# Pacing of block attention under two pair passes of a mixture-of-experts kernel: two end marks moved

## The chip, the cores and the metric

The kernel runs on one core of one Trainium2 chip. The metric is the device time of one execution in microseconds (us); the time before is the median of three runs.

## The reference

Attention over a batch of 4, 8 heads, 768 positions and head dimension 64. Each query sees the keys less than 16 positions away and 24 block summaries (for each block of 32 positions, the largest of K and the mean of V). The result is the x of four experts whose outputs are mixed for each token.

```python
k_sum = k.reshape(B, H, nb, block, D).max(axis=3)
v_sum = v.reshape(B, H, nb, block, D).mean(axis=3)
...
scores_all = np.concatenate([scores_l_m, scores_s], axis=-1)
...
a = a / (np.sum(a, axis=-1, keepdims=True) + 1e-09)
v_all = np.concatenate([v, v_sum], axis=2)
return np.matmul(a, v_all).astype(np.float32)
...
for e in range(E):
    h = np.maximum(x @ w1[e], 0.0)
    out += p[:, e:e + 1] * (h @ w2[e])
```

x has 3072 rows of 512, w1 is 512 by 1024 and w2 1024 by 512 for each expert.

## The kernel before, in words

**Tokens.** The 3072 tokens are eight blocks of 384 (a batch is two blocks). Attention is cut into 64 pieces: 96 queries of four heads, 16 pieces to a batch. Pieces 0 to 7 come ahead of everything else. Pieces 8 to 63 are issued between the matmuls of the experts.

**A piece** is a chain of steps: `load_piece` (line 286, two DMAs, kr and qv), `stage_a` (295, operands split into high and low parts by ACT and POOL), `scores` twice (328: matmuls into psc, masked maximum on DVE, exponential on ACT), `probs` (360, DVE and ACT make aw), `transposed` (386, a DMA transpose), `values` (392, matmuls into px) and `to_x` (429: ACT and DVE make xs, a DMA writes it to DRAM as xd). For each of the batches 1 to 3, `setup_k` (220) and `setup_v` (228) make the block summaries: four K chunks and four V chunks are loaded into two chunk buffers, reduced on DVE, and scaled and turned (`stack_v`, 239).

**Experts.** A plan (line 1071) has six passes: block 0 with experts 0 and 1, block 1 with experts 1 and 0, blocks 0 and 1 together with experts 2 and 3, and then three pair passes, each with one batch and all four experts. In a pair pass each expert has a first stage (`pair_units`, 970: four groups of seven products of six matmuls, whose sums ACT and DVE finish in PSUM while PE goes on) and a second stage (`second`, 907: 144 matmuls into po). In the first pair pass the scaled and split weights are made for the first time (`w1_operands`, 813, and `w2_scaled`, 776, on ACT, POOL and DVE) and stored to DRAM; the second and third pair passes load them from there.

**x of the next pair.** When the last second stage of a pass begins, `x_operands` (453) starts on the x of the next batch. It has four parts of 96 tokens. A part is loaded (xr, into one of the two chunk buffers) once its four xd are written, and ACT, POOL and DVE split it into the 14 operand tiles. The tiles are those that the pass before used, so a tile is free when its last matmul is done.

**The order.** Every step has a key, a place in units of pieces (lines 1033 to 1050). From piece 16 on, piece n has k = n + 1.12; its `stage_a` stands at k - 0.6, its `to_x` at k + 2.3. The summaries of batch b stand at 16b + 1.12 - 2.0 (K) and, for b = 2 and 3, - 1.3 (V). Each pass has an end mark in `ENDS` (line 36), and `advance` issues all steps whose key lies below a mark that moves from the end of the pass before to the end of this one with the work done:

```python
paced = len(experts) * (first_us * (SLOW if pair else 1.0) + second_us)
...
for us, pace in units:
    issue_deferred()
    u += us
    done += us * pace
    advance(pos + (end - pos) * min(1.0, done / paced))

    if nxt < NTB // 2 and u > whole - second_us + 1e-3:
        if parts is None:
            xpair[nxt], parts = x_operands(nxt)
        if parts and written.get((nxt, TB // QB - len(parts))) == 4:
            parts.pop(0)()
```

In a pair pass first_us is 29.4 and second_us 33.264 for one expert and SLOW is 0.6, so paced is 4 x (17.64 + 33.264) = 203.6. The order in which the program issues is a priority only: from line 1067 on a scheduler that models the engines in time places the instructions on each engine's queue, and it may take a later one first where an earlier one isn't ready. Two kinds stay in program order: the K and V chunk loads (line 203) and what was issued before line 1067. Every engine then runs its own queue in order. All DMAs named here are issued by SP. Nearly every instruction carries line 75, that of a helper, so the rows below are told apart by tile names.

Of the kernel before, what the change touches and what calls it, by code (L numbers as in the profile page):

```python
# [32 lines left out]
NEG = -1.0e9 / SCALE  # L33

SHIFT = 1.12
ENDS = (17.52, 25.5, 38.0, 53.0, 68.0, 70.0)
WARM = 11

KEYS = (1.38, 3.85, 1.13, 11.28, 5.91, 6.72, 13.44, 18.09, 21.41, 52.74, 24.82, 23.32, 21.81, 24.25, 59.33, 71.64, 6.83, 9.12)
# [23 lines left out]
def attn_moe(ctx: ExitStack, tc: tile.TileContext, qvL, qv0, v0L, kD, kT, vT, w1L, w2L, dpL, cst, out):  # L63
# [1008 lines left out]
    pos = per  # L1072
    for (tbs, experts), end in zip(plan, ENDS):
        pair = tbs if isinstance(tbs, int) else None
# [89 lines left out]
```

## Time and profile before

| | us |
|---|---|
| runs before: median (lowest to highest) | 1180.99 (1179.97 to 1182.93) |
| profiled execution, device time | 1185.18 |
| its span, first to last instruction | 1183.40 |
| PE busy in the span | 1116.8 (94%) |
| mean granted TensorE clock | 0.972 of full speed |

The page shows one execution. PE is TensorE's matmuls, PEld its weight loads, DVE VectorE, ACT ScalarE, POOL GpSimd, SP the queue that issues the DMAs. In timelines an instruction's idle time ahead of it stands in brackets with what ended it. The first, second and third pair pass begin at 392.08, 693.21 and 945.79 us by PE's first product of each; the last matmul ends near 1179.5.

### The profile page before, as it was taken

To read this page: it belongs to the slowest core of one execution; us is meant where nothing else is said; L and a number is where in the kernel's file an instruction comes from. 1 tells how busy PE (TensorE), PEld (TensorE's weight loads), DVE (VectorE), ACT (ScalarE), POOL (GpSimd) and SP (SyncE) were. 2 spreads that over 40 slices of the span, in tenths; PEclk is the share of its full clock that TensorE was granted. 3 is DMA by queue.
4 is the path that set the end of the run, shared out by engine and by line. 5 is a ranking of instruction groups with operands and counts; after the bars stand their busy time and mean duration, and the time that the engine had idled before them with its cause. 6 is when DMAs were issued, how large, how long until landed. Compare 5 with 4: busy or idle time off the path is not lost.

```text
span 1183.4 us, 19188 instructions
## 1 busy us (share of the span) xinstructions
PE 1116.8 (94%) x6562; PEld 716.4 (61%) x6562; DVE 702.8 (59%) x1767; ACT 595.1 (50%) x1682; POOL 448.2 (38%) x554
## 2 busy tenths in 40 slices
PE   9899698999999879899987999999999999999998
PEld 7888587898897544454544555555555454545453
DVE  5887779875889765665867754453545440414141
ACT  5767466664557777767646654453424230303030
POOL 2588456772736667565544521212111100000000
PEclk9999788999999899899998999999999999999999
DMA  6476656663845767757758354555543132423201
GB/s 237 140 224 177 176 147 184 165 169 92 255 104 151 228 219 228 239 192 208 252 191 227 94 158 125 154 167 155 150 123 83 60 128 67 129 80 116 83 21 54
DMA packets 172179, 181.92 MB, mean 154 GB/s; under 512 B 79664, under 2 KB 115504, under 8 KB 172080
## 3 DMA queue, kind: packets, MB, share of 16 engines
q1 hardware_dynamic: 172080, 180.69, 52.4%
q8 instruction: 51, 0.84, 0.3%
q14 instruction: 48, 0.39, 0.1%
HBM read 129.66 MB, written 34.08 MB: 138 GB/s over the span
## 4 chain that ended last, share of the span: by engine, by line
PE 47%; DMA 2%; DVE 2%; POOL 1%; SPq 1%; ACT 0%; issue 0%; ACTq 0%; DVEq 0%
PE po L75 24%; PE phb L75 10%; PE pha L75 6%; PE phc L75 3%; PE phd L75 3%; PE psc L75 1%; PE px L75 1%; DMA wr<-in_w2L 1%; SPq L75 1%; DMA kch<-in_kT 0%; DMA vch<-in_vT 0%; DVE vsr L75 0%; DVE vmax L75 0%; DMA qv<-in_qvL 0%; POOL qs L75 0%
## 5 line engine op out<-in xcount | busy, mean ns | idle before, releaser
L75 PE MATMUL po<-w,hh 128*128 128x512 f16 (+1 forms) x1536 | 465.1, 384 | 1.3 <-DVE acc L75 1.3
L75 PE MATMUL po<-w,hl 128*128 128x512 f16 (+1 forms) x768 | 293.7, 384 | 0.0
L75 PEld LDWEIGHTS <-w1g 128*128 128x128 f16 x2016 | 197.0, 99 | 157.5 <-issue 28.1
L75 PEld LDWEIGHTS <-hh 128*128 128x128 f16 x1152 | 109.6, 98 | 126.6 <-issue 1.6
L75 PE MATMUL phb<-xh_t,w1g 128*128 128x384 f16 x576 | 166.8, 333 | 14.0 <-DVE phc L75 5.9
L75 PE MATMUL ph<-xh,w 128*128 128x384 f32 x512 | 143.1, 350 | 9.0 <-ACT xh L75 3.7
L75 POOL TENSOR_TENSOR ks<-kr,ks 128x304 fp32r<-128x304 f32 x112 | 100.4, 901 | 131.1 <-ACT ks L75 130.3
L75 POOL TENSOR_TENSOR w<-wr,w 128x512 fp32r<-128x512 f32 (+1 forms) x76 | 101.6, 1343 | 77.8 <-ACT w L75 72.5
L75 ACT ACTIVATE ms<-ms,nb 96x152 f32<-96x152 f32 x256 | 104.2, 414 | 25.2 <-DVE nb L75 24.0
L75 PE MATMUL pha<-xh,w1g 128*128 128x384 f16 x384 | 109.1, 332 | 4.0 <-DVE nb L75 2.5
L75 DVE SCALAR_TENSOR_TENSOR acc<-po,pw,acc 128x512 f32<-128x512 f32 x72 | 51.6, 743 | 90.3 <-PE po L75 90.2
L75 PEld LDWEIGHTS ph<-xh,w 128*128 128x128 f32 x512 | 96.9, 196 | 11.6 <-ACT xh L75 4.0
L75 DVE CUSTOM_DVE_ANT_0 ms<-psc,c_sb 96x152 f32<-96x152 f32 x256 | 69.4, 305 | 57.1 <-PE psc L75 54.2
L75 PEld LDWEIGHTS <-hl 128*128 128x128 f16 x576 | 56.3, 98 | 67.2
L75 PE MATMUL phb<-xl_t,w1g 128*128 128x384 f16 x288 | 96.0, 333 | 0.0
L75 PE MATMUL ph<-xl,w 128*128 128x384 f32 x256 | 88.3, 345 | 0.0
L75 POOL TENSOR_TENSOR v<-qv,v 128x256 f16<-128x256 f32 (+1 forms) x56 | 43.3, 775 | 113.7 <-ACT v L75 88.7
L75 PEld LDWEIGHTS po<-w,hh 128*128 128x128 f32 x384 | 71.1, 190 | 14.5
L75 PE MATMUL psc<-ks,qs 128*96 128x152 f32 x448 | 65.8, 272 | 12.6 <-DVE nb L75 5.4
L75 ACT CAST w<-wr 128x512 fp32r<-128x512 f32 (+1 forms) x100 | 60.7, 615 | 32.8 <-DMA wr<-in_w1L 22.8
L75 DVE TENSOR_TENSOR aw<-ms,aw 96x512 f16<-96x512 f32 x112 | 65.4, 617 | 14.6 <-ACT aw L75 14.4
L75 ACT CAST aw<-ms 96x512 f16<-96x512 f32 x112 | 49.4, 489 | 48.1 <-issue 28.9
(153 smaller groups left out, 1854.6 us busy)
## 6 DMA issues: line engine op xcount, KB each, us to landing
wr<-in_w1L SPq DMA_DIRECT2D x76, 256.0 KB, 3.6
wr<-in_w2L SPq DMA_DIRECT2D x72, 256.0 KB, 3.3
qv<-in_qvL SPq DMA_DIRECT2D x56, 320.0 KB, 3.4
kr<-in_kD SPq DMA_DIRECT2D x56, 256.0 KB, 3.2
w1g<-wdg SPq DMA_DIRECT2D x28, 512.0 KB, 3.5
w<-wd SPq DMA_DIRECT2D x48, 256.0 KB, 2.7
w1g<-wdg SPq DMA_DIRECT2D x28, 384.0 KB, 3.7
wdg<-w1g SPq DMA_DIRECT2D x16, 512.0 KB, 3.7
```

The lines of the kernel that those rows point to most:

```text
L75: ins = getattr(self.engine, name)(*a, **kw)
```

## The change

It moves the end marks of the first and the second pair pass. Nothing else is touched.

```diff
-ENDS = (17.52, 25.5, 38.0, 53.0, 68.0, 70.0)
+ENDS = (17.52, 25.5, 38.0, 51.6, 67.3, 70.0)
```

The first pair pass goes from mark 38.0 to 51.6 where it went to 53.0: 13.6 places where it was 15. The second goes from 51.6 to 67.3 where it went from 53.0 to 68.0. The last step of all, `to_x` of piece 63, has key 63 + 1.12 + 2.3 = 66.42, so the second pass really issues 14.82 places where it issued 13.42. The third pass has no attention in either kernel.

## Rows read from the trace of the kernel before

**Rows 1.** The page of the profile: span, busy time of each engine, and the span in 40 slices of 29.6 us: busy tenths of PE and tenths of the granted TensorE clock.

```profile
span 1183.4 us, 19188 instructions
...
PE 1116.8 (94%) x6562; PEld 716.4 (61%) x6562; DVE 702.8 (59%) x1767; ACT 595.1 (50%) x1682; POOL 448.2 (38%) x554
...
PEclk9999788999999899899998999999999999999999
```

**Rows 2.** Busy time of each engine in the three pair passes (first, second, third), cut at the first matmul of each. Columns: stretch, its length, busy us of PE, PEld, DVE, ACT, POOL (x instructions), granted clock as a share of full speed, DMA share, GB/s.

```profile
392.08:693.21 301.13, 270.17 (x1556) 143.90 (x1556) 199.41 (x477) 200.06 (x551) 168.32 (x213) 0.95 0.68 207
693.21:945.79 252.58, 251.63 (x1514) 136.20 (x1513) 123.28 (x324) 105.26 (x312) 47.61 (x69) 1.00 0.46 131
945.79:1179.50 233.71, 233.68 (x1249) 121.99 (x1247) 68.51 (x124) 42.56 (x96) 0.00 (x0) 1.00 0.28 85
```

**Rows 3.** Who PE waited for in the first pair pass. Columns: us in total, times, longest us.

```profile
PE phb L75 <- DVE phc L75: 5.9, 3, 2.3
PE psc L75 <- DVE nb L75: 5.4, 1, 5.4
PE phb L75 <- ACT phb L75: 4.6, 3, 2.3
PE psc L75 <- POOL qs L75: 2.8, 1, 2.8
PE psc L75 <- DVE hl L75: 2.6, 2, 2.2
PE pha L75 <- DVE nb L75: 2.5, 3, 1.9
```

**Rows 4.** Busy time in two stretches of 10 us of the first pair pass, columns as in Rows 2.

```profile
620.00:630.00 10.00, 3.44 (x18) 2.04 (x20) 7.42 (x23) 6.11 (x16) 2.73 (x3) 0.63 0.75 189
630.00:640.00 10.00, 9.12 (x55) 5.13 (x51) 6.42 (x12) 6.04 (x19) 6.57 (x8) 0.86 0.89 224
```

**Rows 5.** Groups of instructions of the second pair pass that belong to the attention: xcount | busy us, mean ns | idle before, releasers. A piece has two of ks, four of ms with its accumulator, two of aw, and one of each of the others.

```profile
L75 ACT ACTIVATE ms<-ms,nb 96x152 f32<-96x152 f32 x48 | 19.9, 414 | 1.2 <-DVE nb L75 0.7
...
L75 ACT CAST aw<-ms 96x512 f16<-96x512 f32 (+1 forms) x24 | 10.4, 482 | 15.3 <-issue 13.1 <-DVE ms L75 1.1 <-ACT p L75 0.9
...
L75 ACT CAST ks<-kr 128x304 fp32r<-128x304 f32 x22 | 9.8, 445 | 19.7 <-PE psc L75 19.7
...
L75 ACT ACTIVATION_READ_ACCUMULATOR ms<-ms,nb 96x1 f32 x48 | 9.0, 187 | 0.0
...
L75 ACT CAST qs<-qv 128x384 fp32r<-128x384 f32 x11 | 5.6, 510 | 0.0
...
L75 ACT ACTIVATE qv<-qv,vscale 128x256 f32<-128x256 f32 x10 | 5.1, 508 | 14.9 <-DMA qv<-in_qvL 14.9
...
L75 ACT ACTIVATE xs<-px 128x192 f32<-128x192 f32 x14 | 4.6, 332 | 7.2 <-PE px L75 7.2
L75 ACT CAST v<-qv 128x256 f16<-128x256 f32 x11 | 4.5, 408 | 19.6 <-PE px L75 19.6
```

**Rows 6.** The chain that ended last, the stretch of the last expert's second stage: start, us, what.

```profile
1154.65 24.84 PE po L75 x115
```

**Rows 7.** DMA issues of SP around the summary of the last batch (kch and vch are its four K and four V chunks). Columns: start, us, instruction, count; an issue that lasts long was waiting.

```profile
574.85 0.90 SPq L203 DMA_DIRECT2D kch<-in_kT  x2
...
592.82 7.79 SPq L203 DMA_DIRECT2D vch<-in_vT  x4
604.30 0.33 SPq L75 DMA_DIRECT2D wr<-in_w2L  x1
```

**Rows 8.** PE at the start of the fourth expert's first stage: start, us, instruction, and in brackets the idle time before it with what ended it.

```profile
618.03 0.34 PE L75 MATMUL pha<-xh,w1g 128*128 128x384 f16 x1
...
624.57 0.92 PE L75 MATMUL psc<-ks,qs 128*96 128x152 f32 x4 [5.39 <-DVE nb L75]
627.38 0.48 PE L75 MATMUL pha<-xh,w1g 128*128 128x384 f16 x1 [1.88 <-DVE nb L75]
```

**Rows 9.** ACT in the same place.

```profile
624.62 0.72 ACT L75 ACTIVATE wr<-wr,scalew 128x512 f32<-128x512 f32 x1 [3.71 <-DMA wr<-in_w2L]
```

**Rows 10.** SP before the second pair pass: the last write of x (xd) for it and the last two loads of x (xr).

```profile
661.43 0.53 SPq L75 DMA_DIRECT2D xd<-xs  x1
667.58 0.81 SPq L75 DMA_DIRECT2D xr<-xd  x2
```

**Rows 11.** DVE: the last instruction of the split of x for the second pair pass.

```profile
680.04 0.59 DVE L75 TENSOR_TENSOR xl_t<-xr,xh_t 128x192 f16<-128x192 f32 x2
```

**Rows 12.** The split of x: durations ns min/median/max, first and last start us, form.

```profile
L75 DVE TENSOR_TENSOR xr<-xr x48: 335/438/1146, 348.8 to 934.9; 128x192 f32<-128x192 f32 x48
...
L75 POOL TENSOR_TENSOR xl<-xr,xh x36: 542/550/1002, 347.7 to 930.2; 128x192 f16<-128x192 f32 x36
```

**Rows 13.** DMA issues by line: KB each, median us from issue to landing.

```profile
xd<-xs SPq DMA_DIRECT2D x48, 96.0 KB, 2.1
xr<-xd SPq DMA_DIRECT2D x12, 384.0 KB, 3.4
```

**Rows 14.** SP before the third pair pass: the last two writes of x and the last two loads of x.

```profile
908.00 5.56 SPq L75 DMA_DIRECT2D xd<-xs  x2
923.75 0.82 SPq L75 DMA_DIRECT2D xr<-xd  x2
```

## The prediction

> **What bounds the kernel now.** I read the page first: PE is busy for 1116.8 of 1183.4 us and its clock falls only in places [rows 1]. Then the busy time by pass. The second and third pair passes are PE without gaps: 251.63 busy of 252.58 us, 233.68 of 233.71, at full clock. The first is not: 270.17 of 301.13, so 30.96 us idle, at a mean clock of 0.95 [rows 2]. All three do the same expert matmuls, so the difference is attention and loss. A piece costs PE (251.63 - 233.68) / 13 = 1.4 us (the second pass holds 12 sets of scores and 14 of values, so some 13). The first pass has about two pieces more, 2.8 us. So 301.13 - 252.58 - 2.8 = **45.7 us of the first pair pass is loss**: 30 us idle, the rest matmuls at the low clock. Where PE idles for long the clock follows: in the 10 us with 3.44 us of PE work the mean is 0.63, in the next 0.86 [rows 4].
>
> What PE waits for there is mixed: products waiting for DVE and ACT to finish the sums in PSUM (phc 5.9, phb 4.6), and attention: scores or a shared bank waiting for nb, qs and hl, 5.4 + 2.8 + 2.6 + 2.5 = 13.3 us of 30.96, or 43% [rows 3]. No engine is full: DVE and ACT have 199 and 200 us in 301 [rows 2]. They run in order, and in the first stages weight splitting, attention and the PSUM sums share them. So it is a matter of crowding, and there are fewer pieces to crowd after the change.
>
> **The change part by part.** Nothing is removed or added. 1.4 places (15 - 13.6) go from the first pass to the second, each with its steps on five queues: on PE 1.4 us, on ACT 2 x 0.445 + 4 x (0.414 + 0.187) + 2 x 10.4/24 + 0.510 + 0.508 + 0.332 + 0.408 = 5.9 us [rows 5], on SP two loads, a transpose and a write, on DVE and POOL at most (123.28 - 68.51)/13 = 4.2 and 47.61/13 = 3.7 us [rows 2].
>
> PE's own 1.4 x 1.4 = 2.0 us only changes pass: zero. In the second pass ACT's 1.4 x 5.9 = 8.3 us goes beside PE: ACT is at 105 of 253 us, DVE at 123, POOL at 48, and PE loses 0.95 us in the pass [rows 2]. I cost it at nothing. If that cover failed, a piece would cost what one costs now in the first pass, 45.7 / 15 = 3.0 us, and 1.4 pieces 4.3 us: what is gained would come back.
>
> In the first pass the gain isn't shown by any row, so I bound it. Low: only the waits named for attention shrink with the number of pieces, 43% of 45.7 us x 1.4/15 = 1.8 us. High: ACT limits throughout, and all its 8.3 us comes off. A loss is not excluded (the second rival). Between, I let the whole loss go with the number of pieces: 45.7 x 1.4/15 = **4.3 us**. I take it because idle time and slow clock come together [rows 4], while ACT at two thirds busy [rows 2] speaks against the high end.
>
> The summaries of the last batch (keys 47.12 and 47.82) stay in the first pass but move within it: from (47.12 - 38)/15 = 0.608 to 9.12/13.6 = 0.671, and from 0.655 to 0.722. The third expert's second stage runs from 0.587 to 0.75, so they stay inside it; cost zero, and a rival if that fails.
>
> The x of the next pair is complete later. For the second pass the last write moves from (50.42 - 38)/15 = 0.828 to 12.42/13.6 = 0.913; the last second stage begins at 0.837. That is 0.0853 x 203.6 = 17.4 units. Of these 15.6 lie in that stage, whose 33.264 units take 144 x 24.84/115 = 31.1 us [rows 6]: 14.6 us. 1.8 lie in the first stage before it, whose 17.64 units take 233.71/4 - 31.1 = 27.3 us [rows 2]: 2.8 us. Together 17.4 us. Before, the last write was issued at 661.43, the loads waited until 667.58 [rows 10] and the split ended at 680.6 [rows 11], 12.6 us ahead of 693.21 [rows 2]. After, in the same time frame: write 678.8, 2.1 to land, 3.4 for the load [rows 13], and one part's split, between half and all of the 12.2 us that two parts took from the end of their loads' issue (668.4) less that load: 4.4 to 8.8. Sum 688.7 to 693.1: **just in time**, cost zero. For the third pass the shift is 14.82/15.7 - 13.42/15 = 0.0493, x 203.6 x 31.1/33.264 = 9.4 us. The last write there came by 913.6 and the loads only at 923.75 [rows 14]; after: 923.0 + 2.1 + 3.4 + 8.8 = 937.3 against 945.79 [rows 2]. Zero too.
>
> One rule speaks against this. In the split, DVE's subtractions on xr take between 335 and 1146 ns for one form, and POOL's beside them 542 to 1002 [rows 12]. The Trainium skill ("SBUF — State Buffer", section "SBUF: two separate sides") has VectorE instructions with two inputs in SBUF and GpSimd instructions share one port pair by an exclusive lock, and the loser waits for the whole instruction. The spread in those rows agrees. By that rule attention that is now issued beside the last split would lengthen it and the sum would be that of the first rival; by the medians alone it stays at 4.3 us.
>
> **Sum.** Profiled execution 1185.18 (1183.40 of span and 1.78 around it) - 4.3 = 1180.9. It stands 4.2 us above the median of 1180.99, so the median becomes **1176.7 us**.
>
> **The rivals.** *x comes late.* The split's seven two-operand DVE instructions each stand behind one POOL instruction of 0.55 us [rows 12], 3.9 us in all, at the first-to-second change where there is nothing to spare. From 693.1 that makes 697.0, so PE waits up to 3.8 us and the gain is spent: 1176.7 + 3.8 = 1180.5. For it: the slack falls from 12.6 us to nearly none. Against: the split of the third pass ended well ahead, and writes came ahead of their place there.
>
> *The summaries run into the fourth expert* (slower). SP issues the V chunks in order, waiting for the two buffers, from 592.82 to 600.6, and the next weight load only at 604.30 [rows 7]; the fourth expert's first product is at 618.03, and right behind it PE stands 5.39 and 1.88 us [rows 8] while ACT waits 3.71 us for a w2 load [rows 9]. The move is 0.0671 x 203.6 x 31.1/33.264 = 12.8 us at most, 11.9 for K (0.0626). Weight loads for the fourth expert would start at 616 instead of 604, and 11.9 us less the 4.3 gained is **+7.6: 1188.6**. It decides where SP's last V chunk comes after some 611 us, that is, within 7 us of the first product. For it: the chain of this stall begins in that queue. Against: ACT needs these weights only for the second stage, and the scheduler places the casts anew.
>
> *One stall dissolves.* The fourth expert's start loses 7.3 us idle and (1 - 0.63 + 1 - 0.86) x 10 = 5.1 us of clock [rows 4, 8]. If the thinner attention lets it vanish, these 12.4 us take the place of the 4.3: 1181.0 - 12.4 = 1168.6.
>
> *The change does not do what it says:* the scheduler puts the steps where they were. Then nothing moves: 1181.
>
> **How the numbers follow.** Gain of 1.8 to 8.3 us: 0.50 (0.34 over 3.5 us, 0.16 under). One stall dissolves: 0.10. x late, or no effect: 0.14. Summaries collide: 0.26 (0.24 slower by over 3.5 us, 0.02 within). 0.3% is 3.5 us, about what a measurement of this kernel can tell from no change. Faster 0.44, same 0.32, slower 0.24. The likeliest case alone spans 1172.7 to 1179.2. The range goes to both far cases: 1168.5 to 1189.
>
> **What would show it.** Right: the first pass shorter by about 2 + 4.3 us with 13 to 14 sets of scores and about 28 us idle, the second longer by 2 us and still without gaps, PE's first product of each pass with no wait for the split of x. Wrong: idle time over 5 us at the fourth expert's start behind w2 loads, a wait for x at the head of the second or third pass, or new gaps in the second pass. If a stall moves by more than the share of the pieces, the placing by the scheduler matters more than the crowding, and the proportional term is the step that failed.

## The result, and the profile after

| | before | after |
|---|---|---|
| runs: median (lowest to highest), us | 1181.15 (1179.97 to 1182.93) | 1192.36 (1185.21 to 1194.39) |
| profiled execution, us | 1185.18 | 1193.96 |
| its span, us | 1183.4 | 1192.2 |

The ratio of the runs, six of each, is 1.0080 [1.0062, 1.0099]: slower, where 1176.7 was forecast, and 3.4 us above the top of the range. The ratios here and below leave out executions over 1.5% above the fastest of their kernel: one each of after_sum (1205.26 us), after_sum_v3 (6367.13) and before (1203.95).

The page of the kernel after, the lines that answer to [rows 1]:

```profile
span 1192.2 us, 19186 instructions
...
PE 1117.1 (94%) x6562; PEld 717.3 (60%) x6562; DVE 704.2 (59%) x1767; ACT 595.5 (50%) x1682; POOL 447.9 (38%) x554
...
PEclk9999798999999999998989999999999999999999
```

No engine got more to do: PE has 0.3 us more in a span that is 8.8 us longer, so time was lost in waits and clock. Where shows by pass. Busy time in the three pair passes of the kernel after, columns as in [rows 2]:

```profile
391.80:695.26 303.46, 266.84 (x1537) 143.03 (x1536) 196.26 (x459) 196.10 (x534) 164.26 (x208) 0.94 0.63 200
695.26:954.56 259.30, 254.28 (x1534) 137.53 (x1532) 127.80 (x342) 109.77 (x330) 52.35 (x76) 1.00 0.46 134
954.56:1188.40 233.84, 233.68 (x1249) 122.00 (x1247) 68.62 (x125) 42.52 (x96) 0.00 (x0) 1.00 0.27 85
```

The first pass, from PE's first product at 391.83, is 303.43 us: 2.30 longer than before, with 14 sets of scores where it should have become some 6 us shorter. PE is idle for 36.6 us of it, where it was for 31.0. The second is 6.72 longer: 2.65 us more busy time of PE, and 5.02 us idle where there were 0.95. Its extra set of scores and of values (13 and 15 where there were 12 and 14) makes 1.67 of the 2.65: after_dvecopy below has the same sets, no idle time and 253.30 us of work. The rest goes with the stalls. The third is as it was. By experts, the first pass before was 79.95, 74.71, 71.29 and 75.18 us; after, it is 79.51, 69.58, 73.93 and 80.41. So the first two gained 5.6 us, the third lost 2.6 and the fourth 5.2.

Who PE waited for in the second pass (us in total, times, longest), one line and no other:

```profile
PE phb L75 <- ACT phb L75: 4.8, 5, 1.6
```

And in the first pass, where ACT's copy phb had held PE for 4.6 us [rows 3] and nb for more:

```profile
PE phb L75 <- ACT phb L75: 17.6, 6, 6.8
PE pha L75 <- DVE nb L75: 3.6, 3, 1.6
PE phb L75 <- DVE phc L75: 3.4, 3, 1.5
PE psc L75 <- POOL qs L75: 2.8, 1, 2.8
```

The same step heads both lists: ACT's copy of a group's first sum from one PSUM bank, pha, to the next, phb (line 1008). PE can't go on with phb before it. What holds the copy is read from ACT's and PE's timelines, here at the worst place of the second pass (start, us, instruction, idle before):

```profile
785.42 0.51 ACT L75 ACTIVATE qv<-qv,vscale 128x256 f32<-128x256 f32 x1 [2.59 <-DMA qv<-in_qvL]
785.83 0.47 ACT L75 COPY phb<-pha 128x384 f32<-128x384 f32 x1
...
786.35 0.32 PE L75 MATMUL phb<-xh_t,w1g 128*128 128x384 f16 x1 [1.59 <-ACT phb L75]
```

ACT stands at the scaling of a piece's V until its load has landed, and the copy is the next in its queue. The product that PE stands at reads phb and nothing of that load. All five stalls of the second pass stand behind such a wait: at 700.98, 718.58, 766.82, 785.42 and 833.83. In four the copy is the very next instruction, at 700.98 the one after. The Trainium skill ("TensorE: Matmul & The Clock Gate", Part 1) has ScalarE's queue as strictly first in, first out; the order here agrees.

The longest wait of the first pass, 6.8 us, is of the same kind. It stands at the start of the third expert:

```profile
550.32 0.51 ACT L75 ACTIVATE qv<-qv,vscale 128x256 f32<-128x256 f32 x1 [3.12 <-DMA qv<-in_qvL]
550.74 0.47 ACT L75 COPY phb<-pha 128x384 f32<-128x384 f32 x1
...
551.26 0.48 PE L75 MATMUL phb<-xh_t,w1g 128*128 128x384 f16 x1 [6.79 <-ACT phb L75]
```

PE stands there from 544.47. ACT has work until 547.20, then waits 3.12 us for the load of V, and the copy is next. In before PE has no wait for the copy at this place.

The fourth expert of the first pass starts like this (SP's issues, then ACT, then PE):

```profile
598.56 1.67 SPq L203 DMA_DIRECT2D kch<-in_kT  x2
...
600.76 0.90 SPq L75 DMA_DIRECT2D wdg<-w1g  x2
606.18 2.61 SPq L75 DMA_DIRECT2D ks<-ksr  x4
608.88 0.55 SPq L75 DMA_DIRECT2D xd<-xs  x1
609.48 0.91 SPq L203 DMA_DIRECT2D vch<-in_vT  x2
...
611.37 1.41 SPq L75 DMA_DIRECT2D wr<-in_w1L  x2
...
617.42 1.38 ACT L75 ACTIVATE wr<-wr,one 128x512 f32<-128x512 f32 x2 [6.77 <-DMA wr<-in_w1L]
...
621.88 0.47 ACT L75 COPY phb<-pha 128x384 f32<-128x384 f32 x1
...
622.40 0.48 PE L75 MATMUL phb<-xh_t,w1g 128*128 128x384 f16 x1 [6.40 <-ACT phb L75]
```

Read from the bottom: PE waits 6.40 us for the copy, and the copy stands behind ACT's wait of 6.77 us for a w1 load. PE stands from 616.00; 1.42 us of its wait pass until the load has landed, and 4.46 more while ACT does what its queue holds between that wait and the copy (617.42 to 621.88). The load was issued 3.5 us ahead of the expert's first product (614.85), where it was 7.2 before. In front of it on SP's queue stand two V chunks and the four small DMAs that spread the maxima of K (ks from ksr). These wait for DVE's last reduction of the K chunks; SP's waits in this place:

```profile
SPq L75 <- DVE nb L75: 5.3, 2, 5.0
```

(The view names nb; what the spread reads is ksr, and DVE's last reduction of a K chunk ends at 606.15, the spread begins at 606.18. Ahead of that reduction DVE itself had waited 2.52 us for the chunk's load.) The two w1 loads then took 6.0 and 5.8 us to land, with a DMA share of 1.00 from 611 to 617. In kernels without this stall the same loads took from 2.7 (after_sumV) to 5.5 us (before_later), so it is above all the issue that is late. The fourth expert as a whole, before and after:

```profile
618.03:693.21 75.18, 66.92 (x392) 36.04 (x389) 52.76 (x133) 44.71 (x134) 32.73 (x44) 0.93 0.55 150
```

```profile
614.85:695.26 80.41, 68.77 (x398) 37.46 (x397) 58.71 (x148) 45.63 (x134) 31.50 (x44) 0.92 0.51 161
```

Idle went from 8.26 to 11.64 us; the other 1.85 of the 5.23 are matmuls: seven of the summary's own (into pvs and pmx), which came ahead of this expert before, and the lower clock (0.92 against 0.93).

### The profile page after: what moved, and what is told of

Its sections match the earlier page's. It is cut to its first block, busy times and chain, and to the rows that moved or that the text cites. A ratio compares the mean times of both kernels' runs of the same rounds, so it can differ in the third digit from the quotient of the medians.

```text
span 1192.2 us, 19186 instructions
## 1 busy us (share of the span) xinstructions
PE 1117.1 (94%) x6562; PEld 717.3 (60%) x6562; DVE 704.2 (59%) x1767; ACT 595.5 (50%) x1682; POOL 447.9 (38%) x554
```

## The experiments

**The two marks apart, the summaries put back, V loaded by itself.**

```diff
p1_only:   +ENDS = (17.52, 25.5, 38.0, 51.6, 68.0, 70.0)
p2_only:   +ENDS = (17.52, 25.5, 38.0, 53.0, 67.3, 70.0)
after_sum: ENDS of after, and the last batch's summaries as early as before
-steps += [(k - 2.0, setup_k, b), (k - (0.65 if b == 1 else 1.3), setup_v, b)]
+steps += [(k - (2.85 if b == 3 else 2.0), setup_k, b),
+          (k - (0.65 if b == 1 else 2.21 if b == 3 else 1.3), setup_v, b)]
after_v3:  ENDS of after, and V of a piece in a tile of its own
-qv = sb.tile([P, G * QB + G * D], F32, name=f"qv{n}", tag="qv", bufs=2)
+qv = sb.tile([P, G * QB], F32, name=f"qv{n}", tag="qv", bufs=2)
+vv = sb.tile([P, G * D], F32, name=f"vv{n}", tag="vv", bufs=3)
...
-SP.dma_start(qv, qvL[b, i, g])
+SP.dma_start(vv, qvL[b, i, g][:, G * QB :])
+SP.dma_start(qv, qvL[b, i, g][:, 0 : G * QB])
...
-v3 = sb.tile([P, G, D], BF16, name=f"v3_{n}", tag="v3", bufs=3)
+v3 = sb.tile([P, G, D], BF16, name=f"v3_{n}", tag="v3", bufs=1)
```

> Only the first pair pass's end mark moves (51.6, second stays 68.0). Three theories. Late v: ACT runs in order and stands at the scaling of v for the qv load, with the PSUM copy that PE needs behind it; this costs PE only where it falls into a first stage. Collision: the last batch's summaries now run into the fourth expert's first stage of the first pair pass. Crowding, as predicted: loss goes with the number of pieces. Collision and late v: the first pass stays as in the changed kernel, about 303.5 us with some 80 us for the fourth expert, and the total is above before by 4 to 11 us (1185 to 1192), the second pass deciding where between. Crowding: first pass 295, total 1177.

> Only the second pair pass's end mark moves (53.0 kept, 67.3). The number of pieces in each pass is that of before; in the second pass they come some 5% denser. Collision: first pass as before, 301 us, nothing lost at the fourth expert. Late v: the second pass holds 11 or so waits of ACT for qv; those that now fall into first stages cost 1 to 2 us each, so the second pass is 252.6 to 258, by place alone. Crowding: 1181, no change. So total 1181 to 1187.

> The changed kernel with the last batch's summaries put back to the same share of the first pass as before (K 0.608, V 0.655: keys 0.85 and 0.91 earlier). Collision: the fourth expert of the first pass goes from 80.4 back to about 75 us and the total falls by some 5 us to 1187. Late v: nothing changes in the second pass (259 us), and the third expert's 6.8 us wait in the first pass stays unless its place moves. Crowding or x late: no change, 1192.

> The changed kernel with v loaded by a DMA of its own into three buffers (q keeps two), so that the load of v no longer waits for POOL's work on q two pieces before; v3, used only in the first batch, goes from three buffers to one to make room. Late v: ACT's waits for this load nearly vanish, the second pass loses its 5.0 us of idle time (259.3 to about 255) and the third expert's 6.8 us wait in the first pass shrinks; total 1181 to 1186. Collision: the fourth expert's 80 us stays. Crowding: 1192, no change.

All measurements stand in one table. The ratio is that of the runs (ten of a kernel, six of after_dvecopy, four of after_V70) to those of the kernel before on the same chip, with its 95% interval; the lengths are those of the profiled execution: the fourth expert of the first pass (e4), the first and the second pass. One execution can lie anywhere among the runs: that of after_sum, before_v3 and after_sum_dve is the fastest of its ten, that of after_v2 the slowest.

| kernel | ratio | e4 | first | second |
|---|---|---|---|---|
| before | 1 | 75.18 | 301.13 | 252.58 |
| after | 1.0080 [1.0062, 1.0099] | 80.41 | 303.43 | 259.30 |
| p1_only | 1.0036 [1.0009, 1.0063] | 79.23 | 304.34 | 256.49 |
| p2_only | 0.9981 [0.9956, 1.0007] | 75.65 | 300.35 | 251.14 |
| after_sum | 1.0034 [1.0011, 1.0057] | 75.04 | 295.31 | 258.62 |
| after_v3 | 0.9989 [0.9967, 1.0011] | 79.32 | 298.29 | 253.58 |
| after_sum_v3 | 0.9959 [0.9939, 0.9979] | 72.28 | 294.66 | 253.54 |
| before_v3 | 0.9979 [0.9955, 1.0002] | 74.49 | 295.92 | 251.30 |
| after_v2 | 1.0040 [1.0016, 1.0064] | 80.53 | 300.74 | 253.43 |
| before_later | 0.9998 [0.9974, 1.0022] | 75.44 | 296.09 | 252.66 |
| after_dvecopy | 1.0057 [1.0031, 1.0083] | 80.71 | 303.82 | 253.30 |
| after_sumK | 1.0042 [1.0024, 1.0059] | 72.89 | 295.61 | 258.47 |
| after_sumV | 1.0004 [0.9983, 1.0026] | 69.86 | 295.79 | 259.86 |
| after_V70 | 1.0086 [1.0058, 1.0113] | 80.21 | 305.42 | 258.98 |
| after_sum_dve | 1.0002 [0.9985, 1.0020] | 72.81 | 297.32 | 253.30 |
| half | 1.0003 [0.9987, 1.0019] | 70.52 | 298.92 | 251.41 |
| opp | 0.9988 [0.9965, 1.0012] | 68.53 | 302.16 | 249.69 |

The first mark alone makes the kernel slower, the second alone does nothing that can be told. p2_only issues the first pass in the very order of before, so its four experts (78.20, 71.83, 74.67, 75.65) show how far two executions of one order stray: some 3 us for an expert, 1 us for the pass. With the summaries back the fourth expert is at 75.04 and the first pass 8.1 us shorter than in after; the second keeps its loss. With V split the second pass is cured and the fourth expert is not. So there are two separate causes: one at the fourth expert, and one of copies that stand behind ACT's wait for V.

**What the split of V cures.** ACT's waits in the second pass for V's load, in before, after and after_v3:

```profile
ACT qv L75 <- DMA qv<-in_qvL: 14.9, 10, 3.0
```

```profile
ACT qv L75 <- DMA qv<-in_qvL: 20.0, 11, 3.2
```

```profile
ACT vv L75 <- DMA vv<-in_qvL: 13.4, 9, 2.3
```

The waits did not nearly vanish, as after_v3 was expected to show. Before waited nearly as long as after_v3 and lost 0.95 us. What differs is what stands behind the wait. ACT in after_v3, one of its longest waits:

```profile
708.83 0.51 ACT L75 ACTIVATE vv<-vv,vscale 128x256 f32<-128x256 f32 x1 [2.28 <-DMA vv<-in_qvL]
709.25 0.46 ACT L75 COPY p<-phd 128x384 f32<-128x384 f32 x1
709.61 0.87 ACT L75 CAST aw<-ms 96x512 f16<-96x512 f32 x2
...
710.76 0.48 ACT L75 COPY phb<-pha 128x384 f32<-128x384 f32 x1
```

In none of its nine waits is the copy the next instruction or the one after it, and PE doesn't stall. In before it stands so behind three of the ten waits, and one of these is the 0.95 us that PE lost there; in after behind five of eleven, and all five stop PE.

The third expert's stall in the first pass goes with the split too. PE waits 6.1 to 7.5 us for the copy there in all eight kernels that have the first mark at 51.6 and V in one load with Q. In the three with that mark and the split (after_v3, after_sum_v3, after_v2) the longest wait for the copy there is 0.8 us, and in the kernels with the first mark elsewhere 1.9.

**Both cures together, the split in the kernel before, and two buffers for V instead of three** (after_sum_v3 has both edits above; before_v3 has the split with the ENDS of before; after_v2 is after_v3 with bufs=2 for vv).

> The changed kernel with both: summaries put back to the shares of before, and v loaded by its own DMA into three buffers. If the two causes are separate and add: first pass about 295 us as with the summaries alone, second pass about 253.6 as with v alone, so a span near 1177 and a ratio to before some 0.005 below 1. If they are one cause seen twice, or chance: no better than either alone (ratio 0.999 to 1.003).

> Control: the kernel before with v in three buffers by its own DMA. Late v: before had only one wait of 0.9 us in its second pass, so there is nothing to gain there: second pass 251 to 253 us, total within 3 us of before. If separate loading of v helps in itself, wherever the end marks are, the first pass falls by 3 us or more here too (it fell from 303.4 to 298.3 in the changed kernel).

> Control for the third buffer: the changed kernel with v loaded by its own DMA, but two buffers. If the third buffer is what takes the waits away, the second pass stays near 259 us. If the separate DMA (or the new places that every edit gives the instructions on ACT's queue) does it, it is near 254 as with three.

The two cures together have the lowest ratio of the study, 0.9959 [0.9939, 0.9979]. The first two pair passes:

```profile
391.14:685.80 294.66, 265.58 (x1530) 141.73 (x1529) 197.64 (x454) 194.34 (x538) 164.66 (x204) 0.95 0.67 206
685.80:939.34 253.54, 253.54 (x1533) 137.40 (x1532) 127.09 (x342) 109.00 (x328) 52.35 (x76) 1.00 0.48 136
```

In the second pass PE has no idle time left. How much of this needs the new marks is not settled: the split in the kernel before stands at 0.9979 [0.9955, 1.0002], and the intervals overlap. There it makes the profiled first pass 5.2 us shorter, as in the changed kernel (5.1), so by what was expected it may help wherever the marks are; the runs do not show it. after_v2 has the second pass of after_v3 (253.43) and no stall, so a third buffer is not what helps; there too the copy stands behind none of ACT's ten waits, 17.4 us in all. Its profiled execution is longer because its first pair pass began at 398.24 and not at 390.10 as in after_v3: 8.1 of the 10.4 us between their spans (1190.0 and 1179.6) arise ahead of the pair passes, and their cause stays open.

**Is it the lateness of the summaries, of K or of V? And is it the copy on ACT?**

```diff
before_later:  ENDS of before, K at its share of the pass in after (0.671), V at 0.70 (0.722 in after)
+steps += [(k - (1.06 if b == 3 else 2.0), setup_k, b),
+          (k - (0.65 if b == 1 else 0.62 if b == 3 else 1.3), setup_v, b)]
after_dvecopy: ENDS of after, the copy on DVE in the second and third pass
-A.copy(new("b"), o)
+(A.copy if pr == 1 else V.tensor_copy)(new("b"), o)
after_sumK:    after_sum with K alone put back (2.85)
after_sumV:    after_sum with V alone put back (2.21)
```

> The kernel before with nothing changed but the last batch's summaries moved later: K from 0.608 to the 0.671 that it has in the changed kernel, V from 0.655 to 0.70, the latest place ahead of the first step that needs it (0.722 in the changed kernel). Collision: the fourth expert of the first pass goes from 75.2 to 78 to 80 us, the second pass stays at 252 to 254 us, total 3 to 5 us above before. Late v alone, or crowding: no change. Chance placement by the scheduler: any size, either sign, and not at the fourth expert above all.

> The changed kernel with the copy of the first product's sum (pha to phb) given to DVE instead of ACT in the second and third pair pass. Queue order (ACT stands at v's scaling for its load with this copy behind it): ACT's waits for qv stay at some 20 us in the second pass, but PE's waits on ACT's phb go, and the second pass falls from 259.3 to 254 or 255; the first pass stays at 303. If the second pass is longer by the mere amount of attention work, or for another reason: 258 to 260.

> The changed kernel with only the K summary of the last batch put back to 0.608 of the first pass; V stays at 0.722. If SP's wait for the K maxima (ks from ksr), ahead of the fourth expert's w1 loads, makes the collision: fourth expert back to 73 to 76 us, first pass 295 to 297. If it is the V chunks and their reductions on DVE, as the rival put it: it stays at 79 to 81 us.

> The mirror: only the V summary put back to 0.655, K stays at 0.671, so that V comes first. If the V chunks make the collision: fourth expert back to 73 to 76 us. If the K maxima do: it stays at 79 to 81 us.

The copy is the second pass's cause. With it on DVE, PE's time, ACT's waits and the copy itself in the second pass:

```profile
694.11:947.41 253.30, 253.30 (x1533) 137.16 (x1532) 135.35 (x358) 104.74 (x314) 53.67 (x76) 1.00 0.49 137
```

```profile
ACT qv L75 <- DMA qv<-in_qvL: 19.2, 11, 2.3
```

```profile
L75 DVE COPY phb<-pha x16: 552/556/567, 695.7 to 908.0; 128x384 f32<-128x384 f32 x16
```

ACT still waits 19.2 us in 11 places; no wait of PE is left. The copy itself got slower (556 ns, against 467 on ACT in after) and that costs nothing.

For the fourth expert, K alone put back cures it (72.89), and so does V alone (69.86). What it takes, then, is both late. before_later was expected to bring the collision into the kernel before, and did not (75.44). But its first K chunks left SP at 574.73, where they left at 574.85 in before: the key moved and the load did not, so what late K chunks would do in before stays untested. (V at 0.722 can't be had there, since the first `stage_a` of the batch comes ahead of it.) The share of the pass is not the cause even so: after_V70 below has the same two shares, 0.671 and 0.70, and the collision. What tells the two groups apart is SP's order. In after_sumV, where V comes ahead and K behind:

```profile
588.83 2.05 SPq L203 DMA_DIRECT2D vch<-in_vT  x2
606.25 0.42 SPq L75 DMA_DIRECT2D wr<-in_w1L  x1
607.58 0.42 SPq L75 DMA_DIRECT2D wr<-in_w1L  x1
608.64 0.38 SPq L203 DMA_DIRECT2D kch<-in_kT  x1
```

Its first product is at 616.85, so the w1 loads leave 10.6 and 9.3 us ahead. In before_later (first product at 614.54):

```profile
574.73 2.10 SPq L203 DMA_DIRECT2D kch<-in_kT  x2
...
592.04 2.60 SPq L75 DMA_DIRECT2D ks<-ksr  x4
603.61 0.91 SPq L203 DMA_DIRECT2D vch<-in_vT  x2
605.04 0.43 SPq L75 DMA_DIRECT2D wr<-in_w1L  x1
606.28 0.78 SPq L75 DMA_DIRECT2D wr<-in_w1L  x1
```

There the first K chunks leave 39.8 us ahead of the product where after has them at 21.1, so the spread is done by 594.6 and SP free. Every kernel with a long fourth expert (after, p1_only, after_v3, after_v2, after_dvecopy, and after_V70 below: 79.2 to 80.7 us) has the spread of K 8.4 to 9.9 us ahead of the first product, the w1 loads behind it at 3.2 to 4.7, and ACT waiting 5.2 to 6.8 us for them. In the other eleven (68.5 to 75.7 us) the first of these loads leaves 5.6 us ahead or earlier, and ACT waits 2.2 us for one at most, but 3.5 in after_sum_v3, where that wait ends 3.1 us ahead of the product.

**V at another place, both cures without the split, half the change, and the opposite one.**

```diff
after_V70:     ENDS of after, V of the last batch at k - 1.6, its share 0.70; K as in after
after_sum_dve: after_sum with the copy of after_dvecopy
half:          +ENDS = (17.52, 25.5, 38.0, 52.3, 67.65, 70.0)
opp:           +ENDS = (17.52, 25.5, 38.0, 54.4, 68.7, 70.0)
```

> The changed kernel with V's summary of the last batch moved from 0.722 to 0.70 of the first pass, K left at 0.671. If V's place decides: the fourth expert falls from 80 to some 75 us and the first pass from 303.4 to about 296, as with the larger moves. If the pace decides: it stays at 79 to 81 us.

> The changed kernel with the two cures that each touch one cause: summaries back at 0.608 and 0.655, and the copy of the first product's sum on DVE in the second and third pass. If the causes are separate: first pass 295 to 296, second pass 253 to 254, span near 1178, ratio to before 0.995 to 0.998. If not: first pass over 300 or second over 256.

> Half of the change: end marks 52.3 and 67.65, so 14.3 places in the first pass; the summaries come at K 0.638 and V 0.687. Collision by place of V (above 0.70): none here, and crowding gives the first pass 301.1 - 0.7 x 1.4 - 2.1 = 298. Collision as a matter of degree: fourth expert at 77 to 78, first pass 301 to 302. The second pass 253 to 257, by the places of ACT's waits.

> The opposite of the change: end marks 54.4 and 68.7, so 16.4 places in the first pass and 12.0 in the second. Crowding: first pass 301.1 + 1.4 x 1.4 + 4.3 = 307, second 250.6, total 1185. If the first pass stays at 301 to 303 or falls, the number of pieces is not what its loss goes by.

after_V70 keeps the collision (80.21) and the time of after, so V's exact share does not decide. after_sum_dve has the passes of both cures (297.32 and 253.30) and takes away what the change had cost, 1.0002 [0.9985, 1.0020]; the gain over before that was expected did not come. The third expert's stall is still in it (6.66 us), as the copy is on ACT in the first pass; the copy on DVE there too was not tried. half is worth nothing, though its first pass is 298.92: its second, at 251.41, has no idle time at all, and its fourth expert no collision. opp, with more pieces in the first pass, comes out at 302.16 there and not at the 307 that crowding asked for. So the time does not follow the marks in proportion in either direction.

## Why the prediction was wrong

**The view of what bounds the kernel** held: no engine is full, PE loses time where ACT's and DVE's queues make it wait, and the clock falls there (0.91, 0.50 and 0.91 of full in the 10 us from 610, 620 and 630 of after).

**"I cost it at nothing"**, of the pieces moved into the second pass, is the first step that failed. The cover named was the engines' spare time: ACT was busy for 105 of 253 us. Spare time is not what PE needs there. It needs one instruction at one moment, and ACT's queue held it behind a DMA wait. The prediction's own rows showed the wait, 14.9 us for qv [rows 5], and I read it as idle time of an engine with room. The bound given for a failed cover, 4.3 us, came near the 4.07 us of idle time that were added, by luck: it was taken from the first pass's loss per piece, and the loss came at five places in a queue. p2_only, whose pieces stand closer together in the second pass too, has 0.2 us idle. Moving the copy to DVE took it away in the trace, and so did another order on ACT.

**"So they stay inside it; cost zero"**, of the summaries, is the second. They were reckoned by their share of the pass, 0.608 to 0.671 for K. Measured, the first K chunks left SP at 593.73 instead of 574.85, 18.9 us later where 11.9 was the most. In both kernels they leave right behind the loads of piece 48, which SP holds back until POOL has done with a buffer: 7.1 us for kr and 0.9 for qv in after, 2.2 and 1.7 in before. That is 4.1 of the 18.9 us. The rival "the summaries run into the fourth expert" named the place, the queue and the condition (the last V chunk after 611; it left at 617.39), and gave 1188.6. Its mechanism was wrong in part: not weight loads of w2 behind V chunks that wait for buffers, but loads of w1 behind the spread of K's maxima, which waits for DVE, and two V chunks. Its price, 11.9 us on the fourth expert, was too high: 5.2 were measured. It still gave too low a total, since the forecast's gain, subtracted in it, did not come, and the second pass lost as well.

**The crowding term**, 4.3 us for 1.4 places, is not borne out. It has no place for a stall that grows where pieces are fewer, as the third expert's did, from no wait for the copy to 6.8 us. Without the collision the first pass at 13.6 places is 295.31, 295.61, 295.79 and 297.32 (after_sum, after_sumK, after_sumV, after_sum_dve), a mean of 296.0, where before has 301.13 and p2_only, in the same order, 300.35. That is 4.7 us less than the mean of these two, of which 2 are the work that left: some 3 us. But before_later, with all 15 places and only V's summary later, is at 296.09 as well. An effect of the number of pieces can't be told from one of the order that the scheduler happens to find; opp's miss says the same.

**x just in time** was right in what it cost and wrong in its times. Last loads of x and last subtractions for the second and for the third pass in after:

```profile
671.41 0.82 SPq L75 DMA_DIRECT2D xr<-xd  x2
...
685.50 0.62 DVE L75 TENSOR_TENSOR xl_t<-xr,xh_t 128x192 f16<-128x192 f32 x2
...
941.15 0.40 SPq L75 DMA_DIRECT2D xd<-xs  x1
943.15 0.33 SPq L75 DMA_DIRECT2D xr<-xd  x1
...
949.52 0.85 DVE L75 TENSOR_TENSOR xl_t<-xr,xh_t 128x192 f16<-128x192 f32 x2
```

The split for the second pass ended at 686.1, 9.1 us ahead of the first product (688.7 to 693.1 had been worked out, against 693.21). For the third the last write left at 941.15, where 923.0 was expected (931.8 in the time frame of after), and the split ended at 950.4 with 4.2 us to spare. Neither pass begins with a wait of PE. So the rival "x comes late" fell, and the contention that it was built on has no effect on the total: DVE's subtractions on xr take 336 to 1012 ns in after, as spread as in [rows 12], and are done in time. The 15 of these 48 that took over 600 ns ran beside a POOL instruction for 0.69 of their time or more, the other 33 for 0.32 on average. "One stall dissolves" did not come: at the fourth expert's start PE stands 5.39 and 1.88 us in before, 6.40 and 1.44 in after, and 5.85 and 2.97 in after_sum. "The change does not do what it says" fell: 13 sets of scores are in the second pass where there were 12. Of the signs named for being wrong two came: new gaps in the second pass, and idle time at the fourth expert's start, though behind loads of w1 and not of w2.

**What adds up, and what stays open.** By the profiles, 8.8 us = 5.2 in the fourth expert - 2.9 in the other three (the third alone + 2.6) + 6.7 in the second pass - 0.2 ahead of them. By the runs, putting the summaries back takes 1.0080 to 1.0034, the copy on DVE to 1.0057, both to 1.0002: the cures add up, as far as intervals of 0.002 to 0.003 either way can tell. Open is why the scheduler puts the K chunks so much later in after, and in before_later leaves them where they were though their key moved. Open in part is why the runs show less than the profile: after_dvecopy's second pass is 6.0 us shorter than that of after, its runs only 0.0023, or 2.7 us, better. Its profiled execution, 1186.80, lies 4.7 us under the median of its runs. The spread of K on another engine's queue, which would test the cause on SP directly, was not tried.

## What to carry to other kernels

An engine at 40% can still set the pace, if its queue is in order and an instruction that the bottleneck needs stands behind a wait for a DMA: before work is moved beside a "free" engine, look at what that engine waits for and what is next in line. When marks or priorities feed a scheduler, a proportional estimate gives the work that moves and not the order that comes out; read the order, on the DMA-issuing queue first, and keep small DMAs that wait for a computation away from the loads that the next stage needs.

## What was not expected of the hardware

DVE's copy of 128x384 f32 from PSUM to PSUM took 556 ns and ACT's 467. Loads of w1 that were issued 3.5 us ahead of the expert's first product, among V chunks and with a DMA share of 1.00, took 5.8 to 6.0 us to land; the same loads in after_sumV 2.7 to 4.0, in after_sumK 5.1. Executions of one kernel lie further apart than the three first runs let expect: six of after from 1185.21 to 1194.39, and four later sets of 25 to 31 runs of before from 1178.28 upward, with medians of 1183.26 to 1184.63. Where PE does not stall, the passes hardly take part in that: the second is 253.30 us in two kernels and 253.43 to 253.58 in three more, the third 233.68 from its first product to the end of its last matmul in every one. It is in the first pass, where an expert strays by 3 us, and ahead of it: the first pass begins at 392.08 in before and, in the same order, at 389.42 in p2_only. What makes it stray was not found.
